# Second products of a first mixture in float32: one product of 512 columns for each tile in place of two of 256

## The chip, the core and the metric

The kernel runs on one core of a Trainium2 chip. The metric is the device time of one execution in microseconds; lower is better. Times shown are medians of several executions, and one further execution was taken with the hardware profiler on.

## What is computed

Three stages follow one another: a windowed attention, a first mixture of eight experts in which every expert takes exactly 384 tokens, chosen greedily by the order of all scores, and a second mixture with noisy top-2 gates.

```python
def _moe_ref(x, w_gate, w1, w2):          # N = 3072, D = 512, E = 8, F = 1024
    cap = N // E
    logits = x @ w_gate
    order = np.argsort(-logits.flatten())
    ...
    for e in range(E):
        mask = assigned == e
        h = np.maximum(x[mask] @ w1[e], 0.0)
        out[mask] = h @ w2[e]

def _moe2_ref(x, w_gate, w_noise, noise, w1, w2):
    ...
    for e in range(E):
        for k in range(2):
            mask = top2[:, k] == e
            h = np.maximum(x[mask] @ w1[e], 0.0)
            out[mask] += top2_w[mask, k, None] * (h @ w2[e])
```

## The kernel before, in words

Attention runs first, over 24 tiles of 128 tokens, up to about 160 us. Both mixtures then share one program that is written out by a planner. The class Pipe keeps a model clock for each engine (`account`, line 96, gives each instruction an assumed length; for an f32 product it is four times the columns). The main program, `moe1` (line 1441) and `moe2`, issues the big products on PE. After each product it calls `tick` (line 173), which gives every waiting generator a turn if its due time on the model clock of PE has come: loads, splits, the routing chain, the lists, the gathers, the scores. So the order of all engines' queues is fixed when the kernel is built, and it depends on how often `tick` is called. Where the planner expects the operands of the next products to be late, `until` (line 197) either lets the model clock run on, with nothing issued, or, where a tile of PSUM is given as spare, fills the time with spare products of 128 columns on a matrix of ones (written to m, which is overwritten later).

The first mixture serves the experts in the order in which routing settles them; "expert k" is the k-th in that order. For each:

- `route` counts, in a chain of small products (rps) and small DVE steps, how many tokens lie above a threshold, and settles expert after expert. When expert k is settled, `est` is written, and `loads` (line 1017) reads it and issues on SP the loads of its w1 and w2, four pieces of 512 KB each (tiles st, eight buffers; a piece of w2 of the first five experts has to be read by PE before its buffer is loaded again).
- `lists1` makes the list of its tokens: l1pos and slps on PE, sloh and other steps on DVE. `gather1` (line 1293) then gathers the rows (xg) with three indirect transfers from POOL and transposes them, from expert 2 on by DMA transposes on SP (xT), before that by products (tps).
- `split` (line 1065) turns w1 into two f16 parts: squares (junk) and the high part (w_0h to w_3h) on ACT, the low part (w_0l to w_3l) in halves on DVE.
- `mm1` (line 1194) makes the first products: eight tiles (m, three buffers) of 12 products of 384 columns. ACT turns each tile into hT. For experts 0 to 4 hT stays f32. For experts 5 to 7 hT is split in two halves, the second of them on DVE (`halve`, line 1178), and w2 is split as w1 is.
- the second products: for experts 0 to 4 (KF = 5) `mm2_f32` (line 1264), in f32 with the loaded w2 as it is, without a split; for experts 5 to 7 `mm2`, in f16 with 72 products of 512 columns.
- `gate_rows` (line 1327) scales the result (y), writes it to DRAM (rb) and multiplies it with the gate of the second mixture (lg on PE, from yT).

In `mm2_f32` three accumulators (m2f, 128 tokens by 512 columns, f32, one bank of PSUM each) are filled over eight tiles of hT; for each tile of hT and each accumulator there are two products of 256 columns with the same weights (a slice of hT), and a `tick` after each: 48 products for an expert.

The second mixture begins with the expert whose tokens are first known. Its tokens come in two units: unit 0 (three tiles and a half, from the tokens of the first five experts) and unit 1 (three tiles, from all). Unit 0 has 96 first products of 448 columns and then 72 second products of 512 columns and 48 smaller ones. While they run, the scores of the last experts are turned into the choice (rtqpos, cnt), then into the list of unit 1 (slps), whose rows are gathered and transposed for unit 1's first products. The results of unit 0 (z) go out by indirect scatters, which POOL issues in one queue with the gathers.

Of the kernel before, what the change touches and what calls it, by code (L numbers as in the profile page):

```python
# [24 lines left out]
NTOK, DM, E, FF = B * S, H * D, 8, 1024  # L25
KT, FT = DM // 128, FF // 128
# [1237 lines left out]
def mm2_f32(ctx, k, hT):  # L1264

    pipe = ctx.pipe
    ps = [ctx.m1.tile([128, DM], F32, tag="m1", name="m2f") for _ in range(CAP // 128)]
    for ft in range(FT):
        pipe.until(lambda: len(ctx.st.get(2 * k + 1, ())) > ft // 2)
        w2 = ctx.st[2 * k + 1][ft // 2].rearrange("p (k f) -> p k f", k=2)[:, ft % 2]  # L1270
        pipe.wait(w2, hT[ft])
        for a in range(CAP // 128):
            for n in range(0, DM, DM // 2):
                pipe.P.matmul(
                    ps[a][:, n : n + DM // 2], hT[ft][:, 128 * a : 128 * a + 128], w2[:, n : n + DM // 2],
                    start=(ft == 0 and n == 0), stop=(ft == FT - 1 and n > 0),
                )
                pipe.tick()
        ctx.w2_read = FT * k + ft + 1
    return ps  # L1280

# [159 lines left out]
def moe1(ctx):  # L1441
# [39 lines left out]
    for k in range(E):  # L1481
        ps = tile1(ctx)
        if not k:
            pipe.until(lambda: 0 in ctx.gathered)
        pipe.until(lambda: k in ctx.X1 and k in ctx.W, ps)
        xT, ix = ctx.X1[k]
        hT = mm1(ctx, k, xT, CAP, ps)
        m1_done.add(k)
        ys = ctx.wk.tile([128, NA], F32, tag="ys", name=f"ys{k}")
        if k >= KF:  # L1490
            pipe.until(lambda: "comb" in ctx.W[k])
            pipe.V.tensor_scalar(ys, ix, ctx.W[k]["comb"], 1.0 / C_H, op0=ALU.mult, op1=ALU.mult)
        else:
            pipe.V.tensor_scalar(ys, ix, 1.0 / C_H, None, op0=ALU.mult)
            f32 = mm2_f32(ctx, k, hT)
        for a in range(NA):
            ps = mm2(ctx, k, hT, 128 * a, last=a == NA - 1) if k >= KF else f32[a]
            y = ctx.xp.tile([128, DM], F32, tag="pv", name=f"y{k}{a}", bufs=8)
            pipe.S.activation(y, ps, AF.Copy, scale=ys[:, a : a + 1])
            ctx.Y[k, a] = y  # L1500
            pipe.tick()
# [521 lines left out]
```

## Time and profile before

| | us |
|---|---|
| median of 3 runs | 1053.85 |
| lowest and highest | 1053.73, 1054.35 |
| the profiled execution, its own time | 1061.16 |
| its span, first to last instruction | 1059.4 |
| PE busy | 990.7 (94%) |
| DVE busy | 643.4 (61%) |
| ACT busy | 460.4 (43%) |
| POOL busy | 294.0 (28%) |

The profiled execution is 7.3 us longer than the median of the others. PE is TensorE, PEld its weight loads, which overlap it; the length of a product's record is modelled and runs past the start of the next one, so the pace of a stream is read from the starts. A busy engine counts only where the others wait for it. Sections of the page that are used below: the chain that ended last, and answers of the trace for single stretches and tiles. Nearly all instructions of the mixtures have line 68, that of a helper, so tiles' names tell them apart.

### The profile page before, as it was taken

Reading aid. Unit: us, or ns where it says so; the run is one execution under the profiler, and the core shown is the slowest. Engines: PE = TensorE matmul, PEld = TensorE weight load, DVE = VectorE, ACT = ScalarE, POOL = GpSimd, SP = SyncE. Lnnn points to the kernel's source line nnn. Section 1 sums busy time; section 2 is a strip of 40 time slices with the busy share of each in tenths; the row PEclk is TensorE's granted clock in tenths of the full one; section 3 lists DMA queues with packets and bytes.
Section 4 is the critical chain, followed back from the end, with each engine's and each line's share of the span. In section 5 each row is a group of like instructions: output and inputs, shape, how many; then the busy total and the mean of one; then the engine's idle time right before and its main releaser. Section 6 shows DMA issues by size and latency. Waiting matters only on the chain.

```text
span 1059.4 us, 21987 instructions
## 1 busy us (share of the span) xinstructions
PE 990.7 (94%) x8312; PEld 595.4 (56%) x8312; DVE 643.4 (61%) x2096; ACT 460.4 (43%) x817; POOL 294.0 (28%) x471
## 2 busy tenths in 40 slices
PE   7788659999999999999989999999999999999995
PEld 4666556767666675545554454555555555555552
DVE  5787876665765858696856745546455454554220
ACT  2575523544543537888225626044161441613110
POOL 6565423101102114011032223233223332232221
PEclk8998859999999999999999999999999999999998
DMA  8888842656669478967188729559185492563410
GB/s 243 250 256 254 292 149 103 220 161 171 207 212 221 122 189 246 245 202 175 41 222 233 195 103 282 99 126 268 63 237 129 126 266 72 169 120 101 110 60 30
DMA packets 147253, 184.61 MB, mean 174 GB/s; under 512 B 105558, under 2 KB 106070, under 8 KB 145608
## 3 DMA queue, kind: packets, MB, share of 16 engines
q1 hardware_dynamic: 129814, 131.74, 45.9%
q0 software_dynamic: 13872, 45.15, 14.7%
q10 hardware_dynamic: 3458, 6.30, 1.6%
q8 instruction: 66, 1.08, 0.4%
q14 instruction: 43, 0.35, 0.1%
HBM read 127.10 MB, written 32.44 MB: 151 GB/s over the span
## 4 chain that ended last, share of the span: by engine, by line
PE 75%; DVE 9%; DMA 7%; issue 4%; ACT 2%; SPq 2%; POOL 0%; ACTq 0%; DVEq 0%; POOLq 0%
PE m L68 58%; PE m2f L68 10%; PE rps L68 3%; DMA v<-vctx_dram 3%; DMA k<-kT_dram 2%; PE sb L304 1%; SPq L280 1%; DVE sloh L68 1%; PE slps L68 1%; DMA st<-x_dram 1%; PE xb L346 1%; ACT junk L68 1%; SPq L278 1%; DVE hT L68 1%; DMA out_dram<-pv,ts 1%
## 5 line engine op out<-in xcount | busy, mean ns | idle before, releaser
L68 PEld LDWEIGHTS <-hT 128*128 128x128 f16 (+2 forms) x1800 | 143.5, 98 | 161.0 <-issue 5.6
L68 ACT ACTIVATE hT<-m 128x384 f16<-128x384 f32 (+2 forms) x152 | 75.0, 499 | 283.2 <-PE m L68 259.4
L68 DVE SCALAR_TENSOR_TENSOR hT<-m,hT 128x384 f16<-128x384 f32 (+2 forms) x152 | 86.6, 571 | 107.2 <-ACT hT L68 92.6
L68 ACT ACTIVATE junk<-st 128x1024 f16<-128x1024 f32 x108 | 113.6, 1052 | 63.3 <-DMA st<-w_dram 35.0
L68 PE MATMUL m2f<-st,hT 128*128 128x256 f32 x480 | 127.6, 398 | 0.5 <-ACT hT L68 0.5
L68 POOL DMA_INDIRECT out_dram<-pv,ts x47 | 48.4, 1030 | 266.7 <-DVE pv L68 93.6
L68 DVE SCALAR_TENSOR_TENSOR pv<-m,ys,pv 128x512 f32<-128x512 f32 (+2 forms) x47 | 33.5, 714 | 112.0 <-PE m L68 112.0
L68 PE MATMUL m<-xT,w_3h 128*128 128x384 f16 (+2 forms) x384 | 98.3, 337 | 2.2 <-DVE hT L68 2.2
L68 PE MATMUL m<-xT,w_0h 128*128 128x384 f16 (+2 forms) x384 | 96.6, 331 | 3.2 <-DMA xT<-xg 3.2
L68 PE MATMUL m<-xT,w_2h 128*128 128x384 f16 (+2 forms) x384 | 97.3, 333 | 1.7 <-DVE hT L68 1.7
L68 PE MATMUL m<-xT,w_1h 128*128 128x384 f16 (+2 forms) x384 | 96.4, 331 | 0.0
L68 PEld LDWEIGHTS m2f<-st,hT 128*128 128x128 f32 x480 | 83.3, 190 | 10.2 <-ACT hT L68 0.9
L68 PE MATMUL m<-w_2h,hT 128*128 128x512 f16 (+2 forms) x300 | 72.2, 345 | 1.4 <-issue 1.4
L68 PE MATMUL m<-w_3h,hT 128*128 128x512 f16 (+2 forms) x300 | 71.7, 345 | 1.4 <-DVE hT L68 1.4
L68 PE MATMUL m<-w_0h,hT 128*128 128x512 f16 (+2 forms) x300 | 72.1, 346 | 0.0
L68 PE MATMUL m<-w_1h,hT 128*128 128x512 f16 (+2 forms) x300 | 71.5, 345 | 0.0
L68 PE MATMUL m<-xT,w_3l 128*128 128x384 f16 (+2 forms) x192 | 64.4, 335 | 0.0
L68 PE MATMUL m<-xT,w_2l 128*128 128x384 f16 (+2 forms) x192 | 64.0, 333 | 0.0
L68 PE MATMUL m<-xT,w_1l 128*128 128x384 f16 (+2 forms) x192 | 63.6, 331 | 0.0
L68 PE MATMUL m<-xT,w_0l 128*128 128x384 f16 (+2 forms) x192 | 63.5, 331 | 0.0
L68 POOL DMA_INDIRECT xg<-x,rows x54 | 54.2, 1004 | 29.7 <-issue 13.6
L68 POOL DMA_INDIRECT xg<-xr,idx x24 | 24.4, 1017 | 127.6 <-issue 37.6
(336 smaller groups left out, 1874.0 us busy)
## 6 DMA issues: line engine op xcount, KB each, us to landing
st<-w_dram SPq DMA_DIRECT2D x64, 512.0 KB
st<-x_dram SPq DMA_DIRECT2D x64, 512.0 KB
xr<-rb SPq DMA_DIRECT2D x24, 264.0 KB
x<-rb SPq DMA_DIRECT2D x24, 264.0 KB
v<-vctx_dram SPq DMA_DIRECT2D x12, 520.0 KB
v<-vctx_dram SPq DMA_DIRECT2D x24, 260.0 KB
q<-qT_dram SPq DMA_DIRECT2D x12, 512.0 KB
out_dram<-zero ACTq DMA_DIRECT2D x24, 256.0 KB
```

Of the source, the lines that this page charges most:

```text
L68: return f(*args, **kw)
L278: nc.sync.dma_start(behind[:, n : n + 1], flown[-AHEAD])
L280: nc.sync.dma_start(out, src)
L304: nc.tensor.matmul(sc[CH * c : CH * c + CH, hp], q[:, hp, CH * o : CH * o + CH], k[:, :, hp, k0 : k0 + KEYS], start=True, stop=True,)
L346: nc.tensor.matmul(X[hp // 2 if i == G - 1 else 0][CH * c : CH * c + CH, 0 if i == G - 1 else hp // 2, 2 * (hp % 2) : 2 * (hp % 2) + 2, :] ...
```

## The change

```diff
@@ -1270,12 +1270,8 @@
         w2 = ctx.st[2 * k + 1][ft // 2].rearrange("p (k f) -> p k f", k=2)[:, ft % 2]
         pipe.wait(w2, hT[ft])
         for a in range(CAP // 128):
-            for n in range(0, DM, DM // 2):
-                pipe.P.matmul(
-                    ps[a][:, n : n + DM // 2], hT[ft][:, 128 * a : 128 * a + 128], w2[:, n : n + DM // 2],
-                    start=(ft == 0 and n == 0), stop=(ft == FT - 1 and n > 0),
-                )
-                pipe.tick()
+            pipe.P.matmul(ps[a], hT[ft][:, 128 * a : 128 * a + 128], w2, start=(ft == 0), stop=(ft == FT - 1))
+            pipe.tick()
         ctx.w2_read = FT * k + ft + 1
     return ps
```

An accumulator's 512 columns are now one product, 24 for an expert instead of 48 (120 instead of 240 in all), and `tick` is called half as often there. What is computed stays the same. Since the planner's turns fall otherwise, the order of all queues changes from the first expert's second products on; over the whole program PE's order has, apart from m2f, the same instructions and 108 spare products more (221 instead of 113).

The first place is PE's queue between expert 1's second products and expert 2's first (m2f and st_3: last piece of w2; rps: routing; w_0h: the high part of expert 2's w1). Before:

```order
L68 MATMUL m2f<-st_3_3951,hT 128x256 x2
L68 LDWEIGHTS id_227
L68 MATMUL rps_4663<-blk_4659,id_227 15x8
...
L68 LDWEIGHTS w_0h
L68 MATMUL m_4682<-xT_4494,w_0h 128x384
```

With the change:

```order
L68 MATMUL m2f<-st_3_3896,hT 128x512
L68 LDWEIGHTS onesb
L68 MATMUL rps_4549<-flt,onesb 128x8
L68 MATMUL m2f<-st_3_3896,hT 128x512
L68 LDWEIGHTS ones_64
L68 MATMUL m_4567<-ones_64 128x128
...
L68 LDWEIGHTS onesb
L68 MATMUL rps_4629<-flt,onesb 128x8
...
L68 LDWEIGHTS GE_4635
L68 MATMUL rps_4670<-OH_4292,GE_4635 120x64
```

Between the two, 70 spare products now stand, with routing products of five steps among them; before there was none.

The second place is ACT's queue in expert 5's first products (hT: a half from a tile m; junk and jy: squares; w_0h to w_3h: the splits of w2; rb_40: a scaled result). Before:

```order
L68 ACTIVATE hT<-m_6864 128x384
L68 ACTIVATE jy_6901,ssqy_6866<-y_6862 128x512
L68 ACTIVATE junk_0_6955,sq_6952<-st_0_6850 128x1024
L68 ACTIVATE hT<-m_6894 128x384
L68 ACTIVATE w_0h<-st_0_6613,s_11_6948 128x1024
L68 ACTIVATE w_1h<-st_1_6678,s_11_6948 128x1024
L68 ACTIVATE w_2h<-st_2_6781,s_11_6948 128x1024
L68 ACTIVATE w_3h<-st_3_6839,s_11_6948 128x1024
L68 ACTIVATE junk_1_7005,sq_6952<-st_1_6852 128x1024
L68 ACTIVATE rb_40_6964<-y_6837,y_s 128x512
L68 ACTIVATE hT<-m_6985 128x384
```

With the change:

```order
L68 ACTIVATE hT<-m_6838 128x384
L68 ACTIVATE rb_40_6874<-y_6734,y_s 128x512
L68 ACTIVATE hT<-m_6882 128x384
L68 ACTIVATE junk_0_6923,sq_6920<-st_0_6747 128x1024
L68 ACTIVATE w_0h<-st_0_6530,s_11_6916 128x1024
L68 ACTIVATE w_1h<-st_1_6573,s_11_6916 128x1024
L68 ACTIVATE w_2h<-st_2_6651,s_11_6916 128x1024
L68 ACTIVATE w_3h<-st_3_6736,s_11_6916 128x1024
L68 ACTIVATE junk_1_6946,sq_6920<-st_1_6749 128x1024
L68 ACTIVATE hT<-m_6909 128x384
```

The splits stood between the second half and the third; now they stand between the fourth (m_6882) and the fifth (m_6909).

The third place is POOL's queue at the start of the second mixture (xg_0_4 to xg_0_6: the gathers of unit 1; z: unit 0's results). Before:

```order
L68 DMA xg_0_4_8691<-x_61,rows_0_8671 128x528
L68 DMA xg_0_5_8698<-x_61,rows_0_8671 128x528
L68 DMA out_dram<-z_8702,ts_0_8150 3072x512
L68 DMA xg_0_6_8711<-x_61,rows_0_8671 128x528
L68 DMA out_dram<-z_8736,ts_0_8150 3072x512
```

With the change:

```order
L68 DMA xg_0_4_8646<-x_61,rows_0_8626 128x528
L68 DMA out_dram<-z_8650,ts_0_8167 3072x512
L68 DMA xg_0_5_8659<-x_61,rows_0_8626 128x528
L68 DMA xg_0_6_8679<-x_61,rows_0_8626 128x528
L68 DMA out_dram<-z_8685,ts_0_8167 3072x512
```

The scatter of z's second tile moved from behind the second gather to behind the first.

## Rows read from the trace of the kernel before

**Rows 1.** Page, chain that ended last: shares of the span by line.

```profile
PE m L68 58%; PE m2f L68 10%; PE rps L68 3%; DMA v<-vctx_dram 3%; DMA k<-kT_dram 2%; PE sb L304 1%; SPq L280 1%; DVE sloh L68 1%; PE slps L68 1%; DMA st<-x_dram 1%; PE xb L346 1%; ACT junk L68 1%; SPq L278 1%; DVE hT L68 1%; DMA out_dram<-p
```

**Rows 2.** Stretches: us, busy us (instructions) by engine, clock, DMA share, GB/s.

```profile
205.00:232.00 27.00, 27.00 (x227) 17.35 (x226) 17.75 (x69) 14.09 (x29) 0.93 (x9) 1.00 0.50 132
232.00:256.00 24.00, 24.00 (x173) 18.58 (x171) 17.84 (x69) 10.15 (x18) 4.95 (x9) 1.00 0.82 225
```

**Rows 3.** Instructions that write m2f: count, min/median/max ns, first and last start.

```profile
L68 PEld LDWEIGHTS m2f<-st,hT x480: 186/190/200, 182.8 to 399.6; 128*128 128x128 f32 x160
L68 PE MATMUL m2f<-st,hT x480: 377/379/483, 183.0 to 399.8; 128*128 128x256 f32 x160
```

**Rows 4.** Timeline, PE, 231.8 to 243: start, length, what, count.

```profile
231.87 2.32 PE L68 MATMUL m2f<-st,hT 128*128 128x256 f32 x10
...
239.54 1.11 PE L68 MATMUL m2f<-st,hT 128*128 128x256 f32 x4
...
240.88 0.70 PE L68 MATMUL m2f<-st,hT 128*128 128x256 f32 x2
241.51 0.76 PE L68 MATMUL slps<-slr,sloh 128*32 128x12 f16 x24
```

**Rows 5.** Timeline, PE: the spare products ahead of unit 1.

```profile
541.59 1.35 PE L68 MATMUL m<-ones 128*128 128x128 f16 x21
```

**Rows 6.** Chain of waits in order of time: twenty products of 384 columns.

```profile
269.24 3.26 PE m L68 x20
```

**Rows 7.** Timeline, PE: expert 1's slot list, and its rows awaited.

```profile
191.66 0.76 PE L68 MATMUL slps<-slr,sloh 128*32 128x12 f16 x24
...
200.43 0.62 PE L68 MATMUL tps<-id,xg 128*128 128x128 f16 x8 [1.61 <-DMA xg<-xr,idx]
```

**Rows 8.** Timeline, PE: the first product of expert 2's first mixture.

```profile
259.22 0.48 PE L68 MATMUL m<-xT,w_0h 128*128 128x384 f16 x2
```

**Rows 9.** Timeline, SP: transposes for expert 2 and for unit 1.

```profile
247.49 5.94 SPq L68 DMA_TRANSPOSE xT<-xg  x3
...
535.96 8.21 SPq L68 DMA_TRANSPOSE xT<-xg  x3
```

**Rows 10.** Timeline, PE: last scores, slot list of unit 1, its first product.

```profile
513.11 0.35 PE L68 MATMUL lg<-wg2hl,yT 128*128 128x32 f16 x8
...
530.81 0.75 PE L68 MATMUL slps<-slr,sloh 128*128 128x9 f16 x24
...
546.18 0.48 PE L68 MATMUL m<-xT,w_0h 128*128 128x384 f16 x2 [3.24 <-DMA xT<-xg]
```

**Rows 11.** Timeline, DVE: two waits for those PE steps.

```profile
513.51 0.19 DVE L68 TENSOR_REDUCE lg<-lg 128x16 f32<-128x32 f32 x1 [1.26 <-PE lg L68]
...
531.97 0.17 DVE L68 COPY six<-slps 128x9 f32<-128x9 f32 x1 [0.87 <-PE slps L68]
```

**Rows 12.** Timeline, POOL: the scatter of z and the gather behind it.

```profile
535.71 1.02 POOL L68 DMA_INDIRECT out_dram<-z,ts  x1 [0.87 <-DVE z L68]
537.04 0.97 POOL L68 DMA_INDIRECT xg<-x,rows  x1 [0.30 <-issue]
```

**Rows 13.** Timeline, PE: expert 5's sixth tile waits.

```profile
413.48 0.49 PE L68 MATMUL m<-xT,w_2h 128*128 128x384 f16 x2 [1.72 <-DVE hT L68]
```

**Rows 14.** Timeline, ACT: the splits, and the halves behind them.

```profile
405.55 1.15 ACT L68 ACTIVATE w_0h<-st,s 128x1024 f16<-128x1024 f32 x1
...
411.37 0.84 ACT L68 ACTIVATE hT<-m 128x384 f16<-128x384 f32 x2
```

**Rows 15.** Timeline, DVE: a split, and the two halves behind it.

```profile
412.21 0.75 DVE L68 SCALAR_TENSOR_TENSOR w_2l<-st,s,w_2h 128x512 f16<-128x512 f32 x1
412.88 1.02 DVE L68 SCALAR_TENSOR_TENSOR hT<-m,hT 128x384 f16<-128x384 f32 x2
```

**Rows 16.** Stretch behind that wait, columns as in rows 2.

```profile
414.40:417.90 3.50, 3.50 (x13) 1.63 (x11) 2.08 (x5) 0.76 (x3) 2.39 (x6) 0.51 0.96 304
```

## The prediction

> **What bounds the kernel now.** I read the chain that ended last first: two thirds of it are PE's products, the f32 ones of the first mixture (m2f) alone 10% [rows 1]. Then the stretches of the stage that the change touches: PE is busy for all 27.0 us and all 24.0 us of two neighbouring stretches, at full clock [rows 2]. So here time is what PE's queue holds, plus the places where it stands still, and every instruction put into that queue or taken out of it counts in full. DVE, ACT and the DMA queues matter only where PE waits for them: expert 1's rows [rows 7], expert 5's halves [rows 13], the rows of unit 1 [rows 10]. Everything behind unit 1's first product (546 us) has nearly the same order in both kernels and moves as a block.
>
> **The product itself.** Each f32 product is two records in the trace: 480 for 240 products, each with a weight load of 190 ns [rows 3]. Ten records in a row take 2.32 us; without the last one's own 0.379 that is nine steps of 0.216 us [rows 4]. A load of 0.190 fits into a step of 0.216, so it is hidden, and 240 loads fewer are worth nothing while the stream runs. What is left is the fixed part of a step. A product of 384 columns takes 0.163 [rows 6]; one of 128 columns at least a third of that, 0.054, and at most 1.35 / 21 = 0.064 [rows 5], of which I take 0.056, because the 1.35 holds the tail of the last record, which overlaps what comes next. Three times 0.056 is 0.168, so the fixed part is (0.168 - 0.163) / 2 = 0.0025 us. A record of 512 columns should then take 2 x 0.216 - 0.0025 = 0.43, and the 240 records that go save **0.6 us** (between 0 and 1).
>
> The Trainium skill, TensorE: Matmul & The Clock Gate, section Back-to-back issue gap, says that in a stream of load and product pairs the spacing is set by both; its section Weight-path perf modes says that the fast load is not used for fp32. By that rule dropped loads would pay, and I keep it as a rival below; the trace has the load inside the step.
>
> **Where the stream is broken.** Where small products stand between f32 ones, the first f32 load behind them isn't hidden. Four records behind the products of a count take 1.11 - 0.38 = 0.73 us instead of 3 x 0.216 = 0.65; two behind another 0.70 - 0.38 = 0.32 instead of 0.216 [rows 4]: 0.08 to 0.10 us each time. Counted in the two orders, the f32 products of the five experts stand in 99 unbroken groups now and in 79 with the change. The steps of the routing that no longer fall between them stand among f16 products or spares, where I find no such loss. 20 x 0.09 saves **1.8 us** (1.6 to 2.0).
>
> **What the coarser step does to the order.** The generators get a turn after each product, every 0.43 us before and every 0.86 us now. Each step of the routing chain therefore starts later on PE, and by the end of expert 1 the order shows it: 70 spare products stand ahead of expert 2's first product, where there were none. 70 x 0.056 = **3.9 us** more (3.8 to 4.5). Is there a wait there anyway that they only fill? Now the first product starts at 259.22 [rows 8], 17.7 us behind the slot list at 241.51 [rows 4]. Its rows come by gathers and three transposes, issued until 247.49 + 5.94 = 253.43; at unit 1 the product starts 2.0 us behind the end of such issues (546.18 against 544.17) [rows 9, 10]. So expert 2's rows are there at about 255.4 (an estimate from these rows), 13.9 us behind the slot list, and 3.8 us go unused. In the change the slot list stands behind 15 of the 24 products. Nine products (7.7 us), the small steps among them and the spares (some 3 us) and the 3.9 us make 14.6. So the rows are there just before PE is: the spares cost their full length and no wait is added. If the rows were 1.5 us later, 0.8 us would come on top. On SP the third piece of expert 2's w2 now stands ahead of the transposes, waiting for PE's 18th product, 2.6 us behind the slot list; the first transpose now starts 6.0 us behind it, so that wait is covered, by 3.4 us.
>
> **Expert 1's rows.** PE stands still for 1.61 us before the first transposition of expert 1's rows, 8.8 us behind its slot list [rows 7]. Between the two stand 12 products of 256 columns now, and seven of 512 in the change: one product more, 0.86 us, so the wait shrinks to 0.75. **-0.9 us** (-1.6 to 0).
>
> **The last list before the second mixture.** PE waits 3.24 us for unit 1's rows behind 21 spares [rows 5, 10]. The chain to it runs through PE's order: DVE waits 1.26 us for the last scores and 0.87 us for the slot list [rows 11]. In the change the last scores stand behind 54 of unit 0's first products instead of 48 (6 x 0.19 = 1.1 us), the slot list behind 43 of its second products instead of 38 (5 x 0.216 = 1.1 us): the same delay at two places, counted once. From the slot list to unit 1's first product are 15.4 us, and they keep their length: **+1.1 us** (0 to 1.3). That the spares there grow from 21 to 59 costs nothing: behind the list stand five products fewer (1.1 us) and 38 spares more (2.1 us), which leaves 3.24 + 1.1 - 2.1 = 2.2 us of the wait. On POOL one scatter of z moves from behind the second gather to behind the first, and waits for DVE there; two gathers are queued behind it instead of one, and from scatter to next gather it is 537.04 - 535.71 = 1.33 us [rows 12]. The third gather feeds the last transpose, so **+1.3 us** (0 to 2.4, the upper end if the scatter itself is 1.1 us later).
>
> **Expert 5's halves.** The sixth tile waits 1.72 us [rows 13] for the third half of hT, which ACT gives at 411.37, behind four splits from 405.55 on and two more steps [rows 14], and DVE finishes behind a split of its own [rows 15]. Behind it PE's granted clock is 0.51 for 3.5 us [rows 16], the 1.2 GHz level, which costs 1.7 us more. In the change the same four splits and two squares, about 6.6 us, stand between the fourth half and the fifth. PE has three tiles of 12 x 0.163 = 1.95 us and a slot list of 0.7 to fill it, about 6.6 us; ACT's and DVE's own steps for the half (0.8 and 0.5) are left over: a wait of 1 to 2 us again. I take **0** (-3.4 to +2.9).
>
> **Sum.** 3.9 - 0.6 - 1.8 - 0.9 + 1.1 + 1.3 + 0 = +3.0 us, all of it PE's. The profiled execution would go from 1061.16 to 1064.2; the median of the runs shown, 7.3 us below it, from 1053.85 to **1056.9**. A difference of 0.2% (2.1 us) is what can be told from no change here.
>
> **Rivals.**
> 1. The wait at expert 5 goes, and the low clock with it: 1.72 + 1.7 = 3.4 us back, 1053.5, not slower. For it: two halves more are done before the splits start. Against it: the block on ACT is as long as before. It decides at one point: whether the splits start more than 1.5 us before the fourth half. Chance 0.12.
> 2. That wait grows. On DVE four split halves of 0.75 us each [rows 15], with the next expert's list steps among them, now stand ahead of the fifth half: up to 1.2 us more waiting, and a second stretch at half clock for 1.7 us: 1059.8. Chance 0.18.
> 3. The late list costs nothing: the last gather is bound by traffic, not by its issue, and the scores come when they did. Without the two last terms +0.6, 1054.5. For it: the three transposes take 8.21 us to issue [rows 9]. Against it: both of DVE's waits [rows 11]. Chance 0.18.
> 4. The weight loads show: if a record cost its load as well, 240 x 0.190 = 45.6 us would go, 1011.3. All unbroken stretches speak against it [rows 4]. It is the Trainium skill's rule, as named above, taken at its strongest. Chance 0.03.
> 5. The chip runs a 512-column f32 product as pieces of 256, so the 0.6 us stays: 1057.5. Chance 0.04.
>
> **How the numbers follow.** The forecast has the remaining 0.45: 0.35 slower by over 0.2%, 0.07 within, and 0.03 faster for what moves unseen in an order this much changed. Rival 1 gives 0.05 faster and 0.07 same, rival 2 0.18 slower, rival 3 0.03 faster and 0.15 same, rivals 4 and 5 0.03 faster and 0.04 slower. Together: faster 0.14, same 0.29, slower 0.57. The range goes down to rivals 1 and 3 at once (1056.9 - 3.4 - 2.4 = 1051.1) and up to rival 2 with the scatter's upper end and late rows on top (1059.8 + 1.1 + 0.8 = 1061.7).
>
> **What would show it.** In the changed profile: 240 m2f records at steps of 0.43; about 79 groups of them; 70 spares of 0.056 behind expert 1's last f32 product, and no wait behind them; about 0.75 us before expert 1's transposition; unit 1's first product 16.5 us or more behind its slot list; a wait of 1 to 2 us in expert 5's tiles with a low clock after it. A step of m2f far from 0.43, a first product of expert 2 that waits behind the spares, or a second stretch at low clock would prove the sum wrong.

## The result and the profile after

The change made the kernel slower: 1063.45 us, median of five runs (1061.94 to 1066.69), against 1053.73 (1050.83 to 1054.35) for the kernel before, run beside it. The ratio is 1.0106, 95% interval 1.0080 to 1.0132. The profiled execution took 1061.94 with a span of 1060.2. Forecast were 1056.9 us with a range to 1061.7: the sign was right, the size wrong by a factor of three, and the range missed it by 1.8 us.

The two profiled executions alone mislead, since their spans differ by 0.8 us only. Where PE's stages begin shows why (starts of first products in the two traces). At expert 5's first product both stand within 0.5 us of each other, at unit 1's the change is 7.1 us behind (553.27 against 546.18 [rows 10]). What it gains back behind that point it owes to waits and low clock in the profiled execution of before, which the second profile of the same kernel lacks (e1 below). Against that second profile the change takes 7.7 us more from expert 0's first product to unit 1's (391.4 against 383.7). Where the other 2 us of the 9.7 between the medians lie, these profiles don't show.

The page after, lines of parts 1 and 4: PE is the bound as before, with the same share, and m2f has 9% of the chain instead of 10% [rows 1].

```profile
PE 992.6 (94%) x8180; PEld 555.5 (52%) x8180; DVE 641.1 (60%) x2096; ACT 463.1 (44%) x817; POOL 300.5 (28%) x471
...
PE m L68 56%; PE m2f L68 9%; DMA v<-vctx_dram 3%; PE rps L68 3%; DMA k<-kT_dram 3%; DMA out_dram<-z,ts 1%; DMA xT<-xg 1%; PE slps L68 1%; DMA st<-x_dram 1%; PE sb L304 1%; SPq L280 1%; PE xb L346 1%; DMA xg<-xr,idx 1%; DVE w_1l L68 1%; SPq L68 1%
```

m2f after: 240 records in place of 480 [rows 3], and a stream of eight records of 512 columns (timeline, PE). Without the last record's 0.59 and a slow first step of 0.51, six steps take 2.58 us: 0.43 each, as forecast, where two records of before took 0.432 [rows 4].

```profile
L68 PE MATMUL m2f<-st,hT x240: 592/592/697, 183.8 to 400.1; 128*128 128x512 f32 x120
```

```profile
234.45 3.68 PE L68 MATMUL m2f<-st,hT 128*128 128x512 f32 x8
```

The waits of PE at experts 5, 6 and 7 after (timeline, PE). Before, the first had 1.72 us [rows 13]; the other three had no counterpart, but two waits of before are gone, 1.41 us in expert 6's second products and 0.59 just ahead of expert 7's first. Summed over these experts' tiles up to expert 7's second products, PE waits 7.0 us after and 3.7 before.

```profile
417.80 0.48 PE L68 MATMUL m<-xT,w_3h 128*128 128x384 f16 x2 [2.21 <-DVE hT L68]
...
445.26 0.48 PE L68 MATMUL m<-xT,w_2h 128*128 128x384 f16 x2 [0.77 <-DVE hT L68]
...
467.25 0.35 PE L68 MATMUL lg<-wg2hl,yT 128*128 128x32 f16 x8 [1.94 <-DVE y_t L68]
...
481.77 0.80 PE L68 MATMUL m<-xT,w_1h 128*128 128x384 f16 x2 [2.07 <-DVE hT L68]
```

Behind the last two the granted clock falls to 0.57 and 0.65 over stretches of 4 us, near the lower level of 1.2 GHz (stretches after: us, busy us by engine, granted clock, DMA share, GB/s). Together that costs some 3 us, an estimate from 4.00 x 0.43 and 4.00 x 0.35; so the waits are only about half of what the stretch loses against e1.

```profile
468.00:472.00 4.00, 4.00 (x20) 1.57 (x19) 3.56 (x21) 1.79 (x5) 0.42 (x5) 0.57 0.66 196
480.50:484.50 4.00, 2.73 (x15) 1.34 (x15) 2.90 (x7) 3.59 (x8) 0.00 (x0) 0.65 0.93 269
```

What holds PE at 467.25 can be followed on the other engines. On ACT (first fence) four splits of expert 7's w1 stand between the two steps of the second mixture's gates, gu and glw. DVE (second fence) waits 3.41 us for glw, then has eight half splits to do, and reads the scores only at 467.01; PE's next scores overwrite what it reads. Before, glw stood right behind gu (446.62 and 447.67 on ACT).

```profile
455.08 0.24 ACT L68 ACTIVATE gu<-lg 128x48 f32<-128x48 f32 x1 [0.29 <-DVE lg L68]
455.23 1.13 ACT L68 ACTIVATE w_0h<-st,s 128x1024 f16<-128x1024 f32 x1
...
458.34 1.13 ACT L68 ACTIVATE w_3h<-st,s 128x1024 f16<-128x1024 f32 x1
459.38 0.23 ACT L68 ACTIVATE glw<-gw 128x48 f32<-128x48 f32 x1
```

```profile
459.64 0.45 DVE L68 RECIPROCAL gw<-gd 128x48 f32<-128x48 f32 x1 [3.41 <-ACT glw L68]
...
467.01 0.18 DVE L68 TENSOR_REDUCE lg<-lg 128x16 f32<-128x32 f32 x1
```

And at 481.77 PE waits for halves of hT, which stand on ACT behind the four splits of expert 7's own w2:

```profile
476.02 1.13 ACT L68 ACTIVATE w_0h<-st,s 128x1024 f16<-128x1024 f32 x1
...
479.14 1.13 ACT L68 ACTIVATE w_3h<-st,s 128x1024 f16<-128x1024 f32 x1
480.18 0.47 ACT L68 ACTIVATE hT<-m 128x384 f16<-128x384 f32 x1
```

Before, the first of these splits stood 4.4 us ahead of expert 7's first product, which starts at 471.24 (timeline, ACT):

```profile
466.81 1.15 ACT L68 ACTIVATE w_0h<-st,s 128x1024 f16<-128x1024 f32 x1 [0.33 <-DVE s L68]
```

Unit 1 (timeline, PE): slot list, 59 spares, first product. From unit 0's first product to the list are 28.06 us after and 26.98 before (530.81 less 503.83, unit 0's first product in that trace); from the list to unit 1 15.67 and 15.37 [rows 10].

```profile
537.60 0.75 PE L68 MATMUL slps<-slr,sloh 128*128 128x9 f16 x24
547.30 3.47 PE L68 MATMUL m<-ones 128*128 128x128 f16 x59
553.27 0.76 PE L68 MATMUL m<-xT,w_0h 128*128 128x384 f16 x2 [2.51 <-DMA xT<-xg]
```

### The profile page after: what moved, and what is told of

The parts are those of the page before. It is cut to its first block, busy times and chain, and to the rows that moved or that the text cites. A ratio compares the mean times of both kernels' runs of the same rounds, so it can differ in the third digit from the quotient of the medians.

```text
span 1060.2 us, 21719 instructions
## 1 busy us (share of the span) xinstructions
PE 992.6 (94%) x8180; PEld 555.5 (52%) x8180; DVE 641.1 (60%) x2096; ACT 463.1 (44%) x817; POOL 300.5 (28%) x471
## 4 chain that ended last, share of the span: by engine, by line
PE 72%; DMA 11%; DVE 8%; issue 4%; ACT 2%; SPq 2%; POOL 0%; POOLq 0%; DVEq 0%; ACTq 0%
PE m L68 56%; PE m2f L68 9%; DMA v<-vctx_dram 3%; PE rps L68 3%; DMA k<-kT_dram 3%; DMA out_dram<-z,ts 1%; DMA xT<-xg 1%; PE slps L68 1%; DMA st<-x_dram 1%; PE sb L304 1%; SPq L280 1%; PE xb L346 1%; DMA xg<-xr,idx 1%; DVE w_1l L68 1%; SPq L68 1%
## 5 line engine op out<-in xcount | busy, mean ns | idle before, releaser
L68 PE MATMUL m2f<-st,hT 128*128 128x512 f32 x240 | 121.9, 621 | 0.0
L68 POOL DMA_INDIRECT xg<-xr,idx x24 | 27.1, 1128 | 131.1 <-DVE i1c L68 59.0
L68 POOL DMA_INDIRECT pv<-out_dram,tg x47 | 45.7, 972 | 52.7 <-DMA out_dram<-pv,ts 29.1
```

The costliest lines, as they stand in the source:

```text
L68: return f(*args, **kw)
```

## The experiments

Every kernel was timed beside the kernel before. For each profile the table gives three stretches, differences of two starts on PE: I from expert 0's first product to expert 5's first, II from there to expert 7's second products, III from there to unit 1's first product; and where ACT starts to split the w2 of experts 6 and 7, counted from that expert's first product. "Old order" is that of the kernel before.

| | median, us (before beside it) | ratio, 95% interval | I | II | III | splits, us |
|---|---|---|---|---|---|---|
| before, first profile | | | 239.0 | 87.6 | 58.5 | -3.0, -4.4 |
| e1, before | 1053.77 (1054.84) | 0.9985 (0.9962 to 1.0008) | 238.9 | 85.9 | 58.9 | -3.0, -4.4 |
| e15, before | 1060.16 (1060.46) | 1.0002 (0.9979 to 1.0024) | 239.2 | 88.9 | 58.5 | -3.0, -4.4 |
| the change | 1063.45 (1053.73) | 1.0106 (1.0080 to 1.0132) | 238.7 | 93.1 | 59.7 | 3.2, 2.7 |
| e12, the change | 1073.95 (1060.82) | 1.0115 (1.0067 to 1.0163) | 238.6 | 93.3 | 61.5 | 3.2, 2.7 |
| e2, 512, old order | 1054.82 (1054.84) | 0.9990 (0.9970 to 1.0011) | 238.4 | 87.4 | 58.4 | -3.0, -4.4 |
| e3, 256, new order | 1064.90 (1054.84) | 1.0082 (1.0056 to 1.0108) | 244.3 | 91.6 | 59.9 | 3.2, 2.7 |
| e9, route half turns | 1063.55 (1060.82) | 1.0025 (1.0001 to 1.0050) | 244.2 | 85.7 | 58.4 | -4.4, -3.9 |
| e10, all but route | 1063.06 (1060.82) | 1.0021 (0.9993 to 1.0050) | 233.0 | 97.7 | 59.5 | 6.7, 4.8 |
| e13, late part on time | 1055.88 (1060.46) | 0.9953 (0.9933 to 0.9974) | 235.4 | 87.4 | 57.5 | -3.0, -4.4 |
| e14, late at the end | 1070.19 (1060.46) | 1.0087 (1.0056 to 1.0118) | 240.8 | 95.0 | 61.3 | 3.9, 2.5 |

### Is it the product or the order? (e1 to e3)

e1 is the kernel before, unchanged.

> The kernel before, unchanged, for a second profile. The profiled execution shown of it took 1061.16, the median of its runs 1053.7. Theory A (the loss of the change is in the fixed order of the queues; the 7 us between the profiled execution and the median are stalls of that one execution): the time is 1052 to 1055 again, and the second profile lacks some of the stalls of the first: those at 593 (2.22 us and a stretch at half clock), at 755 and at 888 are the candidates. Rival C (executions of one kernel scatter by so much that the 1.0% is chance): the second profile has stalls at other places of the first mixture, and its time lies anywhere between 1051 and 1064.

Theory A's time held, and the candidates fell away as named: the second profile has neither the 2.22 us at 593 nor those at 755 and 888. Expert 5's wait is there again, 1.73 us, but behind it PE stays at full clock, where the first profile had 0.51 [rows 16]:

```profile
416.00 0.48 PE L68 MATMUL m<-xT,w_2h 128*128 128x384 f16 x2 [1.73 <-DVE hT L68]
```

```profile
416.90:420.40 3.50, 3.50 (x24) 2.08 (x23) 2.62 (x7) 1.06 (x4) 2.66 (x5) 1.00 0.99 332
```

e2, in `mm2_f32`, has the new product and keeps the old order on all other engines; on PE the small products that stood between two halves move behind the whole:

```diff
             pipe.P.matmul(ps[a], hT[ft][:, 128 * a : 128 * a + 128], w2, start=(ft == 0), stop=(ft == FT - 1))
+            half = 4.0 * 256 / 2.4
+            pipe.t["p"] -= half
+            pipe.tick()
+            pipe.t["p"] += half + 3.0
+            pipe.ready[ps[a].tensor.name] = (pipe.t["p"], "p")
             pipe.tick()
```

> One product of 512 columns, but the planner's turns are taken twice for each, at the model times of before. On ACT, DVE, POOL and SP the order is that of the kernel before; on PE only the small products that stood between two halves move behind the whole. Theory A (order): the size alone is worth 240 x 2 to 3 ns = 0.6 us and some fewer restarts of the stream (0 to 1.8 us), so 1051.5 to 1053.5, ratio to before 0.998 to 1.000, and no wait at expert 6's scores nor at expert 7's tiles. Rival B (the longer product delays the small steps of routing behind it, and that is the loss): 1060 or more.

Measured: 0.9990, no difference that can be told. Summed over stretch I, from each m2f record to PE's next instruction without the waits, m2f takes 116.3 us in 86 unbroken groups, in e1 118.0 in 99.

e3 keeps the old products in the new order:

```diff
             for n in range(0, DM, DM // 2):
                 pipe.P.matmul(
                     ps[a][:, n : n + DM // 2], hT[ft][:, 128 * a : 128 * a + 128], w2[:, n : n + DM // 2],
                     start=(ft == 0 and n == 0), stop=(ft == FT - 1 and n > 0),
                 )
-                pipe.tick()
+            pipe.t["p"] -= 3.0
+            pipe.ready[ps[a].tensor.name] = (pipe.t["p"], "p")
+            pipe.tick()
```

> Two products of 256 columns as before, but one turn of the planner for each pair; the order of all queues is that of the change. Theory A (order): all of the loss, so 1062 to 1066, and the same waits as in the changed kernel: at expert 6's scores (about 1.9 us), at expert 7's second group of tiles (about 2.1 us), before unit 1 (about 2.5 us), each with half clock behind it. Rival B (size): about 1054. Rival C (chance): waits at other places.

Measured 1064.9 with the waits where the changed kernel has them (2.21, 0.77, 1.93, 2.08 and 2.72 us): the loss comes with the order; e3 has it, e2 doesn't. At the same order the size of the product is worth what was forecast: m2f takes 114.98 us in e3 and 114.39 in the change, 0.59 less. The two losses don't lie at the same places, though. Before expert 2's first product e3 waits 4.38 us and goes on at half clock (0.82 for two products instead of 0.50), where the change waited 0.67; e7's profile has 4.0 there, e4's 3.4. That makes e3's stretch I 5.6 us longer than the change's, and its stretch II is 1.5 us shorter.

```profile
265.11 0.82 PE L68 MATMUL m<-xT,w_0h 128*128 128x384 f16 x2 [4.38 <-DMA xT<-xg]
```

### Single waits taken out of the new order (e4 to e8)

e4 moves one ACT instruction: `glw` ahead of expert 7's four w1 splits.

```diff
+        if i == 2 * (E - 1):
+            pipe.account("s", "activation", (hi, src), {"scale": sj})
+            ctx.kept.append((hi, src, sj))
+        else:
+            S_.activation(hi, src, AF.Copy, scale=sj)
...
     S_.activation(lw, w, AF.Ln)
+    for hi, src, sj in ctx.kept:
+        nc.scalar.activation(hi, src, AF.Copy, scale=sj)
```

> The changed kernel with one instruction of ACT moved: the logarithm of the gates of the second mixture (glw) in expert 6's second products stands ahead of the four splits of expert 7's w1 instead of behind them. All else in all queues is as in the changed kernel. Theory A1 (this block of splits is the root: DVE waits 3.4 us for glw, reads the scores late, PE's score products wait 1.9 us for that, and half clock behind it costs 1.7; and ACT is late for expert 7 for the same reason): the wait of 3.4 on DVE and both waits of PE go, 1063.4 becomes 1056 to 1059. Theory A2 (the two waits have separate causes): only the first goes, 3 to 4 us back, 1059.5 to 1060.5, and expert 7's wait of about 2.1 us stays. Rival (DVE's 6.7 us of splits alone make it late): less than 1 us back.

Measured 1062.11 (before 1054.84; ratio 1.0068, 1.0044 to 1.0092), 2.8 us below e3 of the same comparison, of which 0.6 is the product. That is less than the 3 to 4 us of theory A2, and the intervals of e3 and e4 overlap. The profile decides: DVE's wait for glw and PE's wait at the scores are gone, the one at expert 7 stays with 2.64 us, so the two have separate causes, as A2 says. Stretch II is 89.9.

e5 leaves out the 70 spares ahead of expert 2:

```diff
-                self.P.matmul(spare[:, :128], self.ones, self.ones, start=True, stop=True)
+                if self.quiet:
+                    self.account("p", "matmul", (spare[:, :128], self.ones, self.ones), {})
+                else:
+                    self.P.matmul(spare[:, :128], self.ones, self.ones, start=True, stop=True)
```

> The changed kernel without the 70 spare products ahead of expert 2's first product; all else in all queues is unchanged (the spares compute nothing that is used). Theory R (expert 2's rows come late in the order of the change, 16 to 20 us behind their slot list in the three profiles with that order, and the spares only fill a wait that is there anyway): the time stays within 1.5 us of 1063.5; PE waits 4 to 8 us there, and half clock follows. Rival (as I predicted, the spares cost their own length and the rows are there): about 3.9 us back, 1059.5, and a wait of less than 1 us.

Measured 1.0092 (1.0062 to 1.0121). This interval overlaps the change's, and by the time alone the 3.9 us of the rival aren't excluded; the profile is clearer. PE waits 0.21 to 1.03 us ahead of each routing step between 255 and 260 (2.7 in all), and 3.12 before the product, 17.9 us behind the slot list. That is theory R: the spares take 4.2 us of PE, but only fill a wait that is there anyway; in the change, too, PE still waits 0.67 us behind them.

```profile
258.86 0.35 PE L68 MATMUL rps<-OH,GE 128*120 128x64 f16 x3 [1.03 <-DVE GE L68]
...
263.00 0.82 PE L68 MATMUL m<-xT,w_0h 128*128 128x384 f16 x2 [3.12 <-DMA xT<-xg]
```

e6 issues the transposes of expert 2's rows as third, first, second:

```diff
+                for out, src in (ctx.later[2], ctx.later[0], ctx.later[1]):
+                    ctx.nc.sync.dma_start_transpose(out, src)
```

> The changed kernel with the three transposes of expert 2's rows issued in the order third, first, second, so that none starts before the third gather has landed. Theory T (in two of three profiles with the new order the first transpose, issued 0.2 us behind the start of the third gather, gets ahead of that gather's packets, and the third transpose then starts 9 us behind the gather's issue instead of 5): the first transpose starts about 4 to 5 us behind the end of the third gather's issue, expert 2's first product 16 to 17.5 us behind its slot list in place of 16 to 20, and 1 to 2 us come back on the median: 1061.5 to 1062.5. Rival (the gather is late for the load of w2 issued before it): the third gather lands 9 us behind its issue here too, the two others start later, and it is 1 to 3 us slower than 1063.5.

The third gather then lands within 4 us of the end of its issue, as theory T says, but the product starts 17.9 us behind its list (16.2 in the change, 20.0 in e3), and 1.0094 (1.0057 to 1.0131) is no gain. Why the same order gives 0.6 us of wait in two profiles (the change, e12) and 3.4 to 4.4 in three others (e3, e4, e7) stays open; e12 ran on another chip than those three, so it may be the chip, which wasn't tested. What differs is SP's last transpose: the three take 7.07 us to issue in the change, 11.13 in e3 (timeline, SP, one row of each), the third waiting for its gather; in e4, where that landing is recorded, it comes 15.28 us behind the slot list and the transpose starts at 15.30.

```profile
250.99 7.07 SPq L68 DMA_TRANSPOSE xT<-xg  x3
```

```profile
250.60 11.13 SPq L68 DMA_TRANSPOSE xT<-xg  x3
```

e7 (new order, glw moved as in e4) and e8 (old order, 512 columns) spread the w2 splits of experts 5 to 7 among the halves:

```diff
+        elif i in SPREAD and j:
+            pipe.account("s", "activation", (hi, src), {"scale": sj})
+            ctx.waiting.append((hi, lo, src, sj))
...
     hT.append(h)
+    spread(ctx, 1)
```

> The changed kernel with the logarithm ahead of the splits as before, and with the splits of w2 of the experts 5, 6 and 7 spread out: the second, third and fourth of each follow one half of hT each, on ACT and on DVE, in place of standing in one block ahead of it. Nothing else moves. Theory B (blocks of splits in ACT's queue ahead of the halves make PE's waits): the waits of 2.2 (expert 5), 0.8 (expert 6), 1.9 and 2.1 to 2.6 us (expert 7) and the half clock behind them go, 7 to 9 us: 1055 to 1057. Rival (the splits then come too late for the second products, or the halves are late for another reason): waits of the same size at w2's products, and over 1060.

> One product of 512 columns with the order of before, as in the second experiment, and the same spreading of the splits of experts 5, 6 and 7 (the logarithm stays where it is). Theory B: the wait of 1.7 us at expert 5, which both kernels with the old order have in every profile, goes, and the one of 1.3 us at expert 7's scores may go: 1051.5 to 1053.5, ratio to before 0.997 to 0.999. Rival: the waits of 1.4 us (expert 6's second products) grow since DVE's halves of the splits come later: 1054 to 1057.

Both failed: 1.0143 (1.0101 to 1.0185) and 1.0082 (1.0056 to 1.0107). In e7 the waits at halves shrink at experts 5 and 7 (2.21 to 1.01 and 2.07 to 0.77 us) and grow at expert 6 (0.77 to 1.58), and DVE now waits for late high parts; behind that stand the steps of the next slot list, and PE waits 4.16 us for them (timeline, PE). Spreading the block doesn't pay. What a block costs where it stands this leaves open, since DVE's share of the splits moved with it.

```profile
431.25 0.36 PE L68 MATMUL slps<-slr,sloh 128*32 128x12 f16 x8 [4.16 <-DVE sloh L68]
```

### Which generator is late? (e9 to e15)

The loads tell. SP issues the first piece of w1 of experts 2 to 7 in e1 at 28.7, 37.1, 46.0, 49.1, 40.1 and 43.9 us ahead of that expert's first product, in the change at 27.6, 34.0, 39.5, 41.6, 35.5 and 34.7: the routing chain settles each expert later, and its loads, lists and splits with it. For expert 5 the rows are these (timeline, SP; first e1, whose expert 5 starts at 402.60, then the change, 400.51):

```profile
353.54 3.74 SPq L68 DMA_DIRECT2D st<-w_dram  x4
```

```profile
358.90 2.08 SPq L68 DMA_DIRECT2D st<-w_dram  x4
```

e9 gives that chain alone the extra turn in the middle of a product, e10 all generators but that chain (`tick` here takes a condition on the generator's name):

```diff
+            part = 4.0 * DM / 2.4 / 2
+            pipe.t["p"] -= 1 * part
+            for _ in range(1):
+                pipe.tick(lambda g: g == "route")
+                pipe.t["p"] += part
             pipe.tick()
```

> One product of 512 columns; at the model time of its middle only the routing chain gets an extra turn, all other generators have their turn after the whole product as in the change. The slot lists of experts 2 to 6 then stand within 1.5 us of where they stand in PE's queue before (in the change 5 to 10 us behind that). Theory L (the routing chain, a row of steps that each wait for a turn, is what the coarser turn makes late; loads, lists and splits hang on it and lose their cover): the loss goes, 1053 to 1057, and the stretch from expert 6's second products to expert 7's takes 35 to 37 us instead of 39 to 40.5. Rival M (the other generators' coarser turns, the splits above all, make the blocks): 1061 to 1065.

> The counterpart: the extra turn in the middle goes to every generator but the routing chain. Slot lists of experts 3 to 6 stand 5 to 12 us behind those of before in PE's queue, as in the change. Theory L: most of the loss stays, 1060 to 1066, with waits of PE at experts 5 to 7. Rival M: 1053 to 1057.

By total time neither theory wins (1.0025 and 1.0021). The stretch that was named ahead, from expert 6's second products to expert 7's, took 32.5 us in e9 and 35.6 in e10, so by it e10 has no loss either; e10 loses earlier, between expert 5's second products and expert 6's (43.0 us against 31.8 in e1). Stretch II holds both. With the chain on time stretch II takes 85.7 us and PE has no wait in experts 6 and 7; with the chain late 97.7, 9 to 12 more than with the old order. But against e1 e10 wins 5.9 us in stretch I, which I hadn't expected, and e9 loses 5.3 there: its waits add up to 4.7 us, with half clock behind one of them, and m2f takes 118.7 us in 89 groups, in e10 112.9 in 70.

e11 takes the route's extra turns at the quarters of a product, e12 is the change again.

> As the ninth experiment, with three extra turns for the routing chain in each product of 512 columns, at its quarters. The lists of experts 3 to 7 then stand 3 to 20 us ahead of before in PE's queue. Theory L carried on: waits that the old order still has (expert 1's rows 1 to 2 us, 1.7 at expert 5, 1.4 at expert 6's second products) shrink, 1049 to 1053, faster than both kernels. Rival (what is left of waits comes from elsewhere: splits in front of halves): 1053 to 1057.

> The changed kernel, unchanged, for a second profile. Time 1062 to 1066 as before. If the waits have their cause in the order, PE waits in the same places: 2.2 us at expert 5's fourth group of tiles, 0.8 at expert 6's, 1.9 at the scores of expert 6's second products, 2.1 at expert 7's, 2 to 3 before unit 1; the wait before expert 2's first product may be between 0.5 and 4.5, since it was 0.67 in the first profile and 3.4 to 4.4 in three others with this order.

e11 isn't faster: 1.0057 (1.0024 to 1.0091), stretch I 243.3, stretch II 86.7. The waits of stretch I add up to 5.4 us (2.2 in e1), 3.0 of them in front of routing products, where e1 has none: an earlier chain has PE wait for its steps. e12 waits at the same places for the same times, 2.21, 0.77, 1.94 and 2.08 us, and 0.63 before expert 2. Its median is 10.5 us above that of the change's first runs, and so is the kernel before beside it, by 7.1: e9 to e12 ran on another chip than e1 to e8, and its profiles wait 0.4 us several times around 756, 828 and 896.

e13 and e14 differ from e9 in one line; what decides is k, the expert whose second products run:

```diff
-                pipe.tick(lambda g: g == "route")
+                pipe.tick(lambda g: g != "route" or k > 1)
```

and `k < 2` in e14. e15 is the kernel before beside them.

> One product of 512 columns, the extra turn in its middle for every generator, but for the routing chain only from the third expert (expert 2) on. The slot lists of experts 3 and 4 then stand 5 and 6 us behind those of before in PE's queue, that of expert 5 2 us, and from expert 6 on all queues stand as before. Theory L2 (what costs is that routing is late when the experts with f16 second products begin, since their splits and lists have no cover left; late routing among the f32 experts alone costs nothing, and takes restarts out of the f32 stream): the stretch from expert 5's first product to expert 7's second products takes 85.5 to 87.5 us as with the old order (91.6 to 93.3 in the change), the one from expert 0's to expert 5's first product 233 to 238 (238.9 in the old order); in all 1 to 5 us faster than before on the same chip. Rival (each expert's late list costs where it falls): the first stretch 240 or more, no faster than before.

> The counterpart: the routing chain has the extra turn only for the first two experts. Lists of experts 2 and 3 stand as before, those of experts 4 to 7 4, 5, 8 and 8 us behind. Theory L2: from expert 0's to expert 5's first product 236 to 239 us, from there to expert 7's second products 91 to 96 us; 6 to 10 us slower than before. Rival: no loss (0 to 2 us), since half of the delay of the change is missing.

> The kernel before again, on the chip of the two others, for their stretches side by side: 238 to 239 us from expert 0's to expert 5's first product, 85.5 to 87.6 from there to expert 7's second products, 58.5 to 59 from there to unit 1. If the profile has waits of 0.4 us at PE around 756, 828 and 896, as all four of the last chip and the first profile of this kernel had around 755 and 888, these belong to the chip and not to the kernel.

Theory L2 held, its stretches named ahead, with two misses in size: e14's stretch I took 240.8 us, and e15's stretch II 88.9, since half clock followed expert 5's wait there (some 1.7 us) and PE waited 1.1 us ahead of expert 7's scores. e13 is faster than the kernel before beside it, 0.9953 (0.9933 to 0.9974), 4.6 us by the medians, and by the ratios faster than the change; e14, with the chain late only at the end, has nearly the whole loss, 1.0087 (1.0056 to 1.0118). Rows of timelines show the difference: e13's expert 2 starts 14.5 us behind its slot list without a wait, and expert 7's w2 is split from 461.02 on, 4.4 us ahead of its first product (first fence, PE, then ACT); in e14 it is split from 478.13 on, 2.5 us behind that product, and the waits of the change are back (second fence, PE, then ACT).

```profile
240.53 0.33 PE L68 MATMUL slps<-slr,sloh 128*32 128x12 f16 x7
...
254.98 0.33 PE L68 MATMUL m<-xT,w_0h 128*128 128x384 f16 x1
...
461.02 1.15 ACT L68 ACTIVATE w_0h<-st,s 128x1024 f16<-128x1024 f32 x1 [0.33 <-DVE s L68]
```

```profile
469.82 0.35 PE L68 MATMUL lg<-wg2hl,yT 128*128 128x32 f16 x8 [1.94 <-DVE y_t L68]
...
484.94 0.80 PE L68 MATMUL m<-xT,w_1h 128*128 128x384 f16 x2 [2.93 <-DVE hT L68]
...
478.13 1.13 ACT L68 ACTIVATE w_0h<-st,s 128x1024 f16<-128x1024 f32 x1
```

e13's stretch I takes 3.8 us less than e15's: m2f 114.6 instead of 117.8 us (79 groups instead of 99), waits 0.95 instead of 2.6. Its profile, like e15's, has waits of 0.4 us at PE far behind unit 1; the profiles of the first eight experiments have none there.

## Why the prediction was wrong in size

**The product itself.** Right: steps of 0.43 us, 0.59 us saved at the same order against 0.6 forecast. That dropped weight loads would pay, rival 4, is out: 240 loads fewer are in those 0.59 us. The Trainium skill, TensorE: Matmul & The Clock Gate, section Back-to-back issue gap, has both operations set the spacing in a stream of load and product pairs. The traces here don't agree: with 0.59 us for 240 loads and records, 2.5 ns each, the loads of 0.19 us take no time of their own.

**Restarts.** The count was right (99 and 79 groups), the price too low: m2f fell from 118.0 (e1) to 115.0 us (e3) for 20 groups, 0.15 each instead of 0.09. The slow steps behind the small products, the only ones that I had priced, make 2.0 of the 3.0 us, as forecast. Most of the rest is the step into the small products, which in about half of the groups is longer too, 0.52 us in the change behind its last record of 512 columns, against 0.43. The price depends on which breaks go: in e2, 13 groups fewer bring 1.1 us beyond the product's 0.6, 0.09 each.

**Spares and expert 2's rows.** This step failed: "So the rows are there just before PE is: the spares cost their full length and no wait is added." They only fill a wait (e5). Expert 2 starts on its rows 16 to 20 us behind the slot list in the new order; I had put the rows at 13.9, from the margin at unit 1 (2.0 us). What costs is that the list stands 5.5 us later in expert 1's second products (15.1 us behind their start, 9.6 before). From expert 1's first product to expert 2's the change takes 4.1 us more than before (51.6 against 47.5), close to the 3.9 of the sum: the size was luck, and in e3, e4 and e7 the same stretch takes 54 to 55 us.

**Expert 1's rows.** The wait went altogether, which gives back 1.6 us instead of 0.9.

**The last list before the second mixture.** The list came 1.08 us later, as forecast (1.1). The scatter's 1.3 us aren't confirmed: from the list to unit 1 the change takes 0.3 us more than the first profile of before and none more than e1 (15.72), but its second profile (e12) takes 17.5. The others with this order there (e3 to e7) lie between 15.1 and 18.1, those with the old order (before, e1, e2, e8, e15) between 15.25 and 15.7; why the new order spreads so is open.

**Expert 5's halves.** 2.21 us of wait, inside the 1 to 2.9 that the text allowed for. Of rival 2's 2.9 us only 0.5 came in that profile, where the clock behind the wait stayed full; in e12 the wait is the same and the clock behind it 0.56.

**The step that failed most is one that isn't in the sum.** The text listed three places where PE waits and costed those. "Each step of the routing chain therefore starts later on PE" was seen, and followed only as far as expert 2's spares. It goes on: counted from expert 0's first product, the loads of expert 2 are 2 us later than in e1, and those of experts 4 and 5 7 us: the chain is late, and it takes everything that hangs on it along. When experts 6 and 7 come, their splits no longer lie beside the second products ahead, where ACT has time, but behind the expert's own first product, in front of the halves, and in front of glw: stretch II takes 91.6 to 93.3 us (e3, the change, e12), 5.7 to 7.4 more than in e1. With the old order it takes 85.9 to 88.9, the longer ones with half clock or a wait at expert 7's scores, so the least difference is 2.7. That the late chain is the cause is shown by e13 and e14, which differ in its turns alone, and by e9 and e10; in all four stretch II follows the place of the splits. What a single block of splits costs is shown for the one ahead of glw (e4); for those ahead of the halves it is argued, and e7 and e8 don't show it.

**The trace I summed on.** The profiled execution held about 7 us of waits and low clock from 593 us on that e1's profile doesn't have. None was in the sum, but the sum "profiled execution against profiled execution" came out at 0.8 us, and only the runs told the loss.

## What to carry to other kernels

Where the order of all queues is written out when the kernel is built, an edit of a product's size is above all an edit of that order: build it once with the new product and the old turns, and once the other way round, before its gain is believed. Follow a chain of small steps that starts to run late to the end of everything that hangs on it, and look where its cover ends; here a late chain cost 3 to 12 us at the f16 experts, and among the f32 ones nothing in the two profiles of the change, but 4 to 5 us in e3, e4 and e7, whose expert 2 waited longer for its rows. Then choose where it may be late: with the old turns for all other generators, and for the chain only from the third expert on, the change became a gain of 0.5%.

## What I had not expected of the hardware

The same wait in the same order isn't always followed by the lower clock. Behind expert 5's wait the granted clock was 0.51 in the first profile of before, 1.00 in the second (e1) and 0.58 in the third (e15), after 1.72 or 1.73 us of standing still each time; behind the 2.21 us of the change it was 1.00 in the first profile and 0.56 in the second (e12). That alone moves an execution by about 1.7 us.

```profile
418.60:422.10 3.50, 3.50 (x41) 1.99 (x39) 1.76 (x8) 1.26 (x3) 0.65 (x4) 1.00 0.99 191
```

```profile
419.00:422.50 3.50, 3.50 (x13) 1.53 (x11) 1.22 (x4) 1.28 (x3) 1.31 (x5) 0.56 1.06 202
```

```profile
416.90:420.40 3.50, 3.50 (x15) 1.68 (x13) 1.44 (x4) 0.87 (x3) 2.50 (x6) 0.58 1.02 286
```

The rows are the stretches behind that wait in the change's first and second profile and in e15; the granted clock stands behind the busy times. And executions of the kernel before range from 1050.35 to 1061.20 us beside e1 to e4 alone, so that 0.2% is less than most comparisons here could tell.
